# A table of decay powers made by four GpSimd copies across partitions instead of four on-chip transfers

## The chip, the cores and the metric

One NeuronCore of a Trainium2 chip runs the whole program in one launch. The metric is the device time in microseconds. The kernel before takes 454.82 us, the median of three runs (453.93, 455.42 and 454.82).

## What is computed

The reference is an RWKV-like attention with a decaying state, followed by an MLP with a GELU. For batch 4, 8 heads, 768 tokens and head size 48:

```python
for t in range(S):
    cur = einsum('bhd,bhe->bhde', u * k_t, v_t)
    y[:, :, t] = einsum('bhd,bhde->bhe', r_t, state + cur)
    state = w[None, :, :, None] * state + einsum('bhd,bhe->bhde', k_t, v_t)
x = y.transpose(0, 2, 1, 3).reshape(3072, 384)
h = x @ w_in                                  # 384 x 2048
out = (0.5 * h * (1 + erf(h / sqrt(2)))) @ w_out   # 2048 x 384
```

`w` is one decay per head and channel, so inside a chunk of tokens the decays are powers of `w`.

## The kernel before, in words

**Tiling.** The 768 tokens are six chunks of 128. The eight heads are four pairs, and a pair's two heads lie on partitions 0 to 47 and 64 to 111 of a tile with 112 partitions. A "group" is one chunk of one pair, over all four batches, so there are 24 groups. The four groups of the first chunk (`first_group`, `first_states`) have no state to read; the 20 later ones (`prepare`, `products`, `state`, `finish`) work on two half chunks of 64 tokens and with both orders of the two heads.

**The MLP.** For every chunk 16 blocks j of 128 hidden channels are worked through, 96 steps in all: nine matmuls of 128x512 into `Hp` or `O2` (`moe1`, L697), a gelu twice on ScalarE (L729 rounded, L730 full), their difference on VectorE (L731), and nine matmuls into `O0` to `O2` (`moe2`, L741). Nine, because every float32 factor is split into a high and a low part. The weights are split too, once, in the first steps: a load `raw` (L381), ScalarE's L396 and L399, VectorE's L401, ScalarE's cast `wh` (L405), VectorE's remainder `wl` (L408).

**The table of powers.** `W` (112 partitions, four pairs) holds for every channel w to the powers 0 to 64 (`powers`, L322 to L329), their inverses (`inverse`, L334, one reciprocal for each pair), and a second row of powers for the first chunk (`state_powers`). The later groups need the powers in another layout, and for both orders of the heads: `E[:, p, a, h, i]`. h = 0 has each head's own powers on its partitions. h = 1 has the other head's: those of partitions 64 to 111 go to 0 to 47, and back. `halves` (L365) fills it. E is read by L355 (TensorE transposes of it, from which ScalarE makes `WN2` at L358), by L559 (VectorE, the scaling of a later group's r and k) and by L664 (VectorE, the state).

**What sets the order.** The program gives each piece of work to a planner (`Plan.add`): an engine, an assumed duration, a due time, what it reads and writes. `Plan.run` carries due times back through the users, and `Plan.play` then simulates the engines and hands out, time after time, the ready piece that is due first. So an edit of one piece can move the instructions of every engine. Two of its rules matter here. First, GpSimd's work is kept apart from VectorE's work that is marked `port`: lines 169 to 174 add, to each GpSimd piece with a port, a wait for the last such VectorE piece that was handed out before it. Second, dummy matmuls (`heat`, L306) are put into TensorE's order where the planner foresees a gap before the first step of the MLP. SP's DMA queue is in the planner's order too; each transfer uses one of eight semaphores in turn and waits until the transfer that last used it has landed.

Of the kernel before, what the change touches and what calls it, by code (L numbers as in the profile page):

```python
# [21 lines left out]
B, H, S, D = 4, 8, 768, 48  # L22
# [8 lines left out]
HALF = 64  # L31
LP = 112
# [6 lines left out]
LATER = 10 ** 7  # L39
# [7 lines left out]
SWAP_DUE = 50000  # L47
ROUND = "a"
LOADS = (1, 2, 3, "w0", "w1", 4, "u", "w2", 5)
AT_LOADS, AT_E = 14000, 15000  # L50

SCALE = ("dd", "d", "d", "d")
PRODUCT = ("d", "d", "d", "d")
# [3 lines left out]
class Plan:  # L57
# [16 lines left out]
    def add(self, eng, ns, at, fn, r=(), w=(), port=False):  # L74
        n = len(self.ops)
        deps = set()
        for x in r:
            deps.add(self.writer.get(x))
            self.readers.setdefault(x, []).append(n)
        for x in w:  # L80
            deps.add(self.writer.get(x))
            deps.update(self.readers.pop(x, ()))
            self.writer[x] = n
        deps -= {None, n}
        self.ops.append((eng, ns, at, fn, deps, port or eng == "pool"))
        self.reads.append(set(r))
        self.writes.append(set(w))
        return n

    def dma(self, nbytes, at, fn, r=(), w=()):  # L90
        self.add("sp", nbytes, at, fn, r, w)
# [99 lines left out]
def rwkv_gelu_mlp(tc, rkT, rkv, wuT, uN, wmlp, r, k, vT, w, u, out):  # L191
    nc = tc.nc
    with ExitStack() as ctx:
# [7 lines left out]
        def sb(shape, dt, name, pool=None):  # L201
            return (pool or wk).tile(shape, dt, name=name)
# [19 lines left out]
        W = sb([LP, NP, KEYS + C], F32, "W", pro)  # L222
        WKs = W[:, :, KEYS:]
        E = sb([LP, NP, 2, 2, HALF], F32, "E")
# [27 lines left out]
        add, dma = plan.add, plan.dma  # L252
# [3 lines left out]
        pool = lambda n: 200 + n * 2.1  # L256
# [29 lines left out]
        for dst, src, x in ((diag2, diag, "diag"), (past2, past, "past")):  # L286
            for h in range(2):
                add("act", 245, LATER, lambda dst=dst, src=src, h=h: nc.scalar.copy(
                    out=dst[64 * h:64 * h + 64], in_=src[64 * h:64 * h + 64, 64 - 64 * h:128 - 64 * h]),
                    r=[x], w=[f"{x}2{h}"])  # L290
# [21 lines left out]
        for x in wa:  # L312
            add("act", act(2 * DM), LATER, lambda x=x: nc.scalar.copy(
                out=x.bitcast(F32).rearrange("p (a n) -> p a n", a=2),
                in_=zeros[:, 0:DM].bitcast(F32).unsqueeze(1).to_broadcast([128, 2, DM])), r=["zeros"], w=["wa"])
# [47 lines left out]


        def halves(src, dst, h):  # L365
            W2 = W[src].rearrange("l p (a i) -> l (p a) i", a=2)[:, :, 32:32 + HALF]
            nc.sync.dma_start(E[dst].rearrange("l p a h i -> l (p a) h i")[:, :, h], W2)

        every = [f"W{p}" for p in PAIRS] + ["P", "WKs"]
        for i, (src, dst, h) in enumerate(((slice(0, LP), slice(0, LP), 0), (slice(48, 64), slice(48, 64), 1),  # L370
                                           (slice(0, D), slice(64, LP), 1), (slice(64, LP), slice(0, D), 1))):
            dma(60000, AT_E, lambda src=src, dst=dst, h=h: halves(src, dst, h), r=every, w=[f"E{i}"])
        EVERY = [f"E{i}" for i in range(4)]
        add("pe", 560, LATER, lambda: flip(lambda p: E[:, p, 1].rearrange("l h i -> l (h i)")), r=EVERY + ["ident"], w=["O0"])
        add("act", 400, LATER, flipped(WN2), r=["O0"], w=["WN2"])
# [70 lines left out]
        def first_group(gi, at, XX, XB, y, YB):  # L446
# [8 lines left out]
            for i, e in enumerate(halves):  # L455
                nb = NB // len(halves)
                bs = slice(i * nb, i * nb + nb)
                mul = nc.vector.tensor_tensor if e == "d" else nc.gpsimd.tensor_tensor
                add("dve" if e == "d" else "pool", dve(256 * nb) if e == "d" else pool(256 * nb), LATER,
                    lambda mul=mul, bs=bs, nb=nb: mul(  # L460
                        out=t[:, :, bs], in0=T[gi][:LP, :, bs],
                        in1=W[:, p, 0:C].unsqueeze(1).unsqueeze(1).to_broadcast([LP, 2, nb, C]), op=ALU.mult),
                    r=["P", f"W{p}", f"T{gi}"], w=[f"{TR}{b}" for b in range(bs.start, bs.stop)], port=True)
# [545 lines left out]
```

## Time and profile before

| what | value |
| --- | --- |
| median of three runs | 454.82 us |
| the profiled execution | 453.82 us, its span 452.1 us |
| TensorE busy | 440.6 us, 97% of the span |
| VectorE busy | 229.4 us, 51% |
| ScalarE busy | 186.7 us, 41% |
| GpSimd busy | 68.5 us, 15% |

The span runs from the first to the last instruction; the rest of the execution's time lies around it. The shares are means over stages that differ: VectorE and ScalarE are nearly full in the first 80 us, while the weights are split, and have much room after that. In the slices of the page TensorE's row reads 7 9 8 8 and then 9 throughout.

### The profile page before, as it was taken

The page shows a single profiled execution, that of the slowest core. Times are in us where ns is not written, and L with a number is a line of the kernel's source. Part 1 is how long each engine was busy: PE and PEld are TensorE (multiplying, and loading weights), DVE is VectorE, ACT ScalarE, POOL GpSimd, SP SyncE. Part 2 cuts the span into 40 slices and gives each one's busy share as a digit, 9 for nine tenths or more (in the row PEclk, how much of TensorE's full clock was granted, in tenths as well). Part 3 has the DMA queues.
Part 4 walks back from the last instruction along what each step waited for, and adds up shares of the span by engine and source line. Part 5 has one row for each costly group of instructions (what it writes and reads, how often), then busy time and mean ns, then how long its engine had stood idle before and what let it go on. Part 6 is the DMA issues. An engine that isn't in the chain of part 4 may idle for free.

```text
span 452.1 us, 10289 instructions
## 1 busy us (share of the span) xinstructions
PE 440.6 (97%) x4525; PEld 379.4 (84%) x4525; DVE 229.4 (51%) x345; ACT 186.7 (41%) x333; POOL 68.5 (15%) x91
## 2 busy tenths in 40 slices
PE   7988999999999999999999999999999999999995
PEld 6767878888888888888888888888888888888885
DVE  7988979876353538253454545445425411211111
ACT  9998998533232223222233222323223222322221
POOL 1233011223101211102202202112022000000000
PEclk9999999999999999999999999999999999999999
DMA  8987864335031234030321411302503000100002
GB/s 300 362 336 226 292 222 174 112 113 171 1 113 45 68 113 146 26 106 5 113 80 73 131 54 59 112 25 87 171 1 112 15 0 13 70 1 1 1 0 75
DMA packets 15426, 46.60 MB, mean 103 GB/s; under 512 B 3664, under 2 KB 4048, under 8 KB 15376
## 3 DMA queue, kind: packets, MB, share of 16 engines
q1 hardware_dynamic: 15376, 45.88, 30.9%
q8 instruction: 37, 0.61, 0.6%
q14 instruction: 13, 0.11, 0.1%
HBM read 38.73 MB, written 4.72 MB: 96 GB/s over the span
## 4 chain that ended last, share of the span: by engine, by line
PE 78%; ACT 8%; DVE 6%; DMA 5%; issue 2%; POOL 1%; SPq 0%; ACTq 0%; POOLq 0%
PE Hp L697 36%; PE O L741 34%; DMA E<-W 2%; PE Y L607 2%; ACT wh L405 2%; ACT wa L396 2%; PE Y L635 2%; PE A L615 2%; ACT wb L399 1%; DVE wb L401 1%; DMA raw<-in_wmlp_dram 1%; PE Y L741 1%; PE A L624 1%; DMA T<-in_rkT_dram 1%; ACT gh L729 1%
## 5 line engine op out<-in xcount | busy, mean ns | idle before, releaser
L697 PE MATMUL Hp<-xx,wh 128*128 128x512 f32 x570 | 157.0, 383 | 0.4 <-ACT gf L730 0.4
L731 DVE TENSOR_TENSOR gl<-gf,gh 128x512 fp32r<-128x512 f32 x92 | 67.8, 737 | 139.5 <-ACT gf L730 138.8
L729 ACT ACTIVATE gh<-Hp 128x512 fp32r<-128x512 f32 x91 | 54.4, 598 | 190.2 <-PE Hp L697 190.1
L697 PEld LDWEIGHTS Hp<-xx,wh 128*128 128x128 f32 x570 | 105.4, 189 | 16.5 <-ACT gf L730 0.8
L741 PE MATMUL O<-gh,wh 128*128 128x512 f32 (+1 forms) x276 | 74.5, 377 | 3.3 <-ACT gh L729 2.5
L697 PE MATMUL Hp<-xx,wl 128*128 128x512 f32 x285 | 77.4, 379 | 0.0
L741 PE MATMUL O<-gl,wh 128*128 128x512 f32 (+1 forms) x276 | 74.1, 376 | 0.0
L741 PE MATMUL O<-gh,wl 128*128 128x512 f32 (+1 forms) x276 | 73.9, 375 | 0.0
L741 PEld LDWEIGHTS O<-gh,wh 128*128 128x128 f32 x276 | 51.6, 189 | 12.8 <-ACT gh L729 4.5
L697 PEld LDWEIGHTS Hp<-xx,wl 128*128 128x128 f32 x285 | 53.8, 189 | 7.6
L741 PEld LDWEIGHTS O<-gl,wh 128*128 128x128 f32 x276 | 51.2, 189 | 7.2 <-issue 0.3
L741 PEld LDWEIGHTS O<-gh,wl 128*128 128x128 f32 x276 | 51.3, 189 | 6.8
L730 ACT ACTIVATE gf<-Hp 128x512 f32<-128x512 f32 x95 | 56.4, 594 | 0.0
L562 POOL TENSOR_TENSOR Nb<-Nb 128x384 f32<-128x384 f32 x20 | 20.1, 1007 | 127.0 <-DMA Nb<-in_rkv_dram 81.3
L559 DVE TENSOR_TENSOR Tb<-Tb,E 112x1024 f32<-112x1024 f32 x20 | 25.0, 1252 | 3.0 <-DMA Tb<-in_rkT_dram 3.0
L565 POOL TENSOR_TENSOR Nb<-Nb,WN 128x384 f32<-128x384 f32 x20 | 20.8, 1038 | 28.1 <-DVE wl L408 17.3
L664 DVE SCALAR_TENSOR_TENSOR Sb<-Sa,E,A 48x192 f32<-48x192 f32 x40 | 16.5, 413 | 14.9 <-PE A L624 14.3
L434 ACT CAST xx<-Y 112x512 fp32r<-112x512 f32 x15 | 8.9, 592 | 36.3 <-PE Y L635 36.3
L568 POOL TENSOR_TENSOR Nb<-Nb,u_sb 128x384 f32<-128x384 f32 x20 | 21.3, 1064 | 6.7 <-DVE gl L731 6.7
L571 DVE TENSOR_REDUCE cs<-Nb 128x8 f32<-128x384 f32 x20 | 11.0, 552 | 21.4 <-POOL Nb L568 20.5
L396 ACT ACTIVATE wa<-raw 128x768 f16<-128x768 bf16 x16 | 18.9, 1182 | 0.2 <-DMA raw<-in_wmlp_dram 0.2
L399 ACT ACTIVATE wb<-raw 128x768 int32<-128x768 uint32 x16 | 18.6, 1187 | 0.2 <-DVE wl L408 0.2
(124 smaller groups left out, 371.1 us busy)
## 6 DMA issues: line engine op xcount, KB each, us to landing
raw<-in_wmlp_dram SPq DMA_DIRECT2D x16, 767.8 KB, 6.1
Nb<-in_rkv_dram SPq DMA_DIRECT2D x20, 576.0 KB, 5.5
Tb<-in_rkT_dram SPq DMA_DIRECT2D x20, 512.0 KB, 3.9
out_dram<-raw SPq DMA_DIRECT2D x5, 768.0 KB, 3.6
T<-in_rkT_dram SPq DMA_DIRECT2D x4, 512.0 KB, 5.2
xx<-x SPq DMA_DIRECT2D x30, 64.0 KB, 4.2
N<-in_rkv_dram SPq DMA_DIRECT2D x4, 384.0 KB, 7.0
out_dram<-raw SPq DMA_DIRECT2D x2, 256.0 KB, 3.9
```

The source lines that it names most:

```text
L396: add("act", 930, LATER, lambda: nc.scalar.activation(out=a.bitcast(F16).rearrange("p (n t) -> p n t", t=2)[:, :, 1], in_=top.bitcast(BF16 ...
L399: add("act", 815, LATER, lambda: nc.scalar.activation(out=b, in_=rest.bitcast(U32), func=AF.Copy, scale=2.0 ** -13), r=[R_], w=[B_])
L559: add("dve", 1140, LATER, lambda: nc.vector.tensor_tensor(out=flat, in0=flat, in1=E[:, p, 0].rearrange("l h i -> l (h i)").unsqueeze(1).to ...
L562: add("pool", pool(DM), LATER, lambda: nc.gpsimd.tensor_tensor(out=n[:, 0], in0=n[:, 0], in1=n[:, 1], op=ALU.mult), r=[NK], w=[NR])
L565: add("pool", pool(DM), LATER, lambda: nc.gpsimd.tensor_tensor(out=kn, in0=kn, in1=WN2[:, p].rearrange("s j d -> s (j d)").unsqueeze(1).to ...
L568: add("pool", pool(DM), LATER, lambda: nc.gpsimd.tensor_tensor(out=n[:, 0], in0=n[:, 0], in1=u_sb[:, p, :].unsqueeze(1).to_broadcast([C, N ...
L664: add("dve", 430, at, lambda l=l, x=x: nc.vector.scalar_tensor_tensor(out=out[quarter(1 - x)], in0=src[l], scalar=E[l, p, 1, h, 32:33], in ...
L697: nc.tensor.matmul(dst, lhsT=wt[j][:, 0, k_ * 128:(k_ + 1) * 128], rhs=pairs(x[:, a, k_, :]), start=start and k_ == ks[0], stop=stop and k ...
L729: add("act", 480, LATER, lambda: nc.scalar.activation(out=high, in_=dst, func=AF.Gelu, scale=256.0), r=[H_], w=[GH])
L730: add("act", 480, LATER, lambda: nc.scalar.activation(out=gf, in_=dst, func=AF.Gelu, scale=256.0), r=[H_], w=["gf"])
L731: add("dve", dve(512), LATER, lambda: nc.vector.tensor_tensor(out=low, in0=gf, in1=high.bitcast(F32), op=ALU.subtract), r=["gf", GH], w=[G ...
L741: nc.tensor.matmul(dst[:, a:b], lhsT=wt[j][:, 1, d * 128:(d + 1) * 128], rhs=pairs(gt)[:, a // 2:b // 2], start=(j == 0 and n == 0), stop= ...
```

## The change

The four transfers of L367, given to SP's queue with a fixed due time, become four GpSimd copies. Each reads `W` and writes one part of E, across partitions where h = 1. The second part is copied from a wider block, partitions 32 to 63 in place of 48 to 63, so that it overlaps the third on 32 to 47; the third therefore waits for the second. The last two change places. The pieces have no due time of their own but get it from their users, and an assumed duration of 700 ns.

```diff
-AT_LOADS, AT_E = 14000, 15000
+AT_LOADS = 14000
...
         def halves(src, dst, h):
-            W2 = W[src].rearrange("l p (a i) -> l (p a) i", a=2)[:, :, 32:32 + HALF]
-            nc.sync.dma_start(E[dst].rearrange("l p a h i -> l (p a) h i")[:, :, h], W2)
+            W2 = W[src].rearrange("l p (a i) -> l p a i", a=2)[:, :, :, 32:32 + HALF]
+            return nc.gpsimd.tensor_copy(out=E[dst, :, :, h], in_=W2)
 
         every = [f"W{p}" for p in PAIRS] + ["P", "WKs"]
-        for i, (src, dst, h) in enumerate(((slice(0, LP), slice(0, LP), 0), (slice(48, 64), slice(48, 64), 1),
-                                           (slice(0, D), slice(64, LP), 1), (slice(64, LP), slice(0, D), 1))):
-            dma(60000, AT_E, lambda src=src, dst=dst, h=h: halves(src, dst, h), r=every, w=[f"E{i}"])
+        for i, (src, dst, h) in enumerate(((slice(0, LP), slice(0, LP), 0), (slice(32, 64), slice(32, 64), 1),
+                                           (slice(64, LP), slice(0, D), 1), (slice(0, D), slice(64, LP), 1))):
+            add("pool", 700, LATER, lambda src=src, dst=dst, h=h: halves(src, dst, h), r=every,
+                w=[f"E{i}"] + ["E1"] * (i == 2))
```

The planner then hands out a different order on every engine. Lines behind the edit are one higher in the new file (L471 is L472, L697 is L698); the text keeps the old numbers.

GpSimd, at the start of the program, before. `ident` is the identity for transposes, `N` the first chunk's k and v, `Nb` a later group's.

```order
L279 AFFINE_SELECT ident<-ones 128x128
L517 TENSOR_TENSOR N_107<-N_107,WN 128x384
L517 TENSOR_TENSOR N_108<-N_108,WN 128x384
L517 TENSOR_TENSOR N_109<-N_109,WN 128x384
L517 TENSOR_TENSOR N_110<-N_110,WN 128x384
L562 TENSOR_TENSOR Nb_111<-Nb_111 128x384
L565 TENSOR_TENSOR Nb_111<-Nb_111,WN_92 128x384
```

The same place of GpSimd now:

```order
L279 AFFINE_SELECT ident<-ones 128x128
L367 COPY E<-W 32x8x64
L367 COPY E<-W 112x8x64
L367 COPY E<-W 48x8x64 x2
L518 TENSOR_TENSOR N_107<-N_107,WN 128x384
L518 TENSOR_TENSOR N_108<-N_108,WN 128x384
L518 TENSOR_TENSOR N_109<-N_109,WN 128x384
L518 TENSOR_TENSOR N_110<-N_110,WN 128x384
L563 TENSOR_TENSOR Nb_111<-Nb_111 128x384
L563 TENSOR_TENSOR Nb_112<-Nb_112 128x384
```

The four copies stand ahead of the four decay products of the first chunk. In the new program's list of waits the first copy waits for VectorE's L421 and the second for VectorE's L401; the four products wait in turn for the copies, L408 of the first weight block, and the first and the second L559.

VectorE, from the scaling of the second group to the first weight block, before:

```order
L334 RECIPROCAL W<-W 112x64 x3
L460 TENSOR_TENSOR Ts_99<-T_93,W 112x2x256 x2
L466 TENSOR_TENSOR RK_104<-T_94 112x512
L460 TENSOR_TENSOR Ts_100<-T_94,W 112x1024
L490 COPY_PREDICATED Am_113<-past,A 128x1024
L466 TENSOR_TENSOR RK_105<-T_95 112x512
L466 TENSOR_TENSOR RK_106<-T_96 112x512
L460 TENSOR_TENSOR Ts_101<-T_95,W 112x1024
L435 TENSOR_TENSOR x_123<-O_72,x_123 112x512
L490 COPY_PREDICATED Am_114<-past,Y 128x1024
L460 TENSOR_TENSOR Ts_102<-T_96,W 112x1024
L421 TENSOR_TENSOR Am_116<-diag,cs_120 128x512
```

The same place of VectorE now:

```order
L334 RECIPROCAL W<-W 112x64 x2
L461 TENSOR_TENSOR Ts_100<-T_94,W 112x1024
L467 TENSOR_TENSOR RK_105<-T_95 112x512
L491 COPY_PREDICATED Am_113<-past,A 128x1024
L461 TENSOR_TENSOR Ts_101<-T_95,W 112x1024
L467 TENSOR_TENSOR RK_106<-T_96 112x512
L491 COPY_PREDICATED Am_114<-past,Y 128x1024
L436 TENSOR_TENSOR x_123<-O_72,x_123 112x512
L334 RECIPROCAL W<-W 112x64
L461 TENSOR_TENSOR Ts_102<-T_96,W 112x1024
L422 TENSOR_TENSOR Am_116<-diag,cs_120 128x512
L402 ISA wb_134<-wb_134,wa_132 128x1536
```

Three reciprocals that ran in one go are now a pair and a single one, and the last stands behind the second L490.

TensorE, from the last scores of the first chunk to the first steps of the MLP, before. `O_70` takes the transposes of E, `A` the states' gains, `Hp` and `O_72` the first two steps.

```order
L498 MATMUL O_72<-x_123,spread 128x512 x2
L355 MATMUL O_70<-ident,E 128x112 x4
L306 MATMUL Hp<-zeros 128x512
L504 MATMUL O_72<-Am_115,N_109 48x128 x8
L498 MATMUL O_71<-x_123,spread 128x512 x2
L526 MATMUL A<-N_107 48x48 x8
L526 MATMUL A<-N_108 48x48 x8
L504 MATMUL O_71<-Am_116,N_110 48x128 x8
L697 MATMUL Hp<-xx_121,wh_74 128x512
```

The same place of TensorE now:

```order
L306 MATMUL Hp<-zeros 128x512 x5
L505 MATMUL O_72<-Am_115,N_109 48x128 x8
L499 MATMUL O_71<-x_123,spread 128x512 x2
L355 MATMUL O_70<-ident,E 128x112 x4
L505 MATMUL O_71<-Am_116,N_110 48x128 x8
L698 MATMUL Hp<-xx_121,wh_74 128x512
L698 MATMUL Hp<-xx_121,wl_78 128x512
L698 MATMUL Hp<-xx_121,wh_74 128x512 x2
L698 MATMUL Hp<-xx_121,wl_78 128x512
L698 MATMUL Hp<-xx_121,wh_74 128x512
L527 MATMUL A<-N_107 48x48 x8
L527 MATMUL A<-N_108 48x48 x8
```

The transposes of E have moved behind one L504 and stand directly ahead of the last one, and the first 16 gain products have moved behind the first six L697.

## Rows read from the trace of the kernel before

**Rows 1.** Busy time by stretch: stretch, length, PE, PEld, DVE, ACT, POOL, clock, DMA share, GB/s
```profile
8.00:16.00 8.00, 7.87 (x91) 6.75 (x90) 7.86 (x10) 7.69 (x27) 0.00 (x0) 1.00 1.03 408
23.60:78.00 54.40, 50.72 (x553) 41.69 (x550) 48.39 (x65) 50.82 (x67) 11.29 (x13) 1.00 0.72 252
78.00:96.00 18.00, 17.89 (x320) 15.37 (x319) 13.22 (x20) 10.00 (x16) 5.53 (x7) 1.00 0.29 83
96.00:440.00 344.00, 343.89 (x3395) 299.35 (x3394) 145.50 (x226) 101.90 (x187) 46.93 (x60) 1.00 0.21 66
```

**Rows 2.** TensorE's waits, 23.6 to 96 us (us in total, times, longest)
```profile
PE O L741 <- ACT gh L729: 2.5, 4, 1.0
PE O L741 <- ACT gf L730: 0.8, 1, 0.8
PE Hp L697 <- ACT gf L730: 0.4, 1, 0.4
```

**Rows 3.** Timeline of TensorE, 18 to 31 us (start, length, instruction)
```profile
19.27 0.55 PE L355 MATMUL O<-ident,E 112*128 112x112 f32 x4
19.59 0.48 PE L306 MATMUL Hp<-zeros 128*128 128x512 f32 x1
...
21.95 0.92 PE L526 MATMUL A<-N 128*48 128x48 f32 x32
22.71 1.04 PE L504 MATMUL O<-Am,N 128*48 128x128 f32 x16
23.68 0.48 PE L697 MATMUL Hp<-xx,wh 128*128 128x512 f32 x1
...
25.18 0.93 PE L526 MATMUL A<-N 128*48 128x48 f32 x32
26.03 0.48 PE L697 MATMUL Hp<-xx,wh 128*128 128x512 f32 x1
...
28.49 0.81 PE L697 MATMUL O<-xx,wl 128*128 128x512 f32 x3
29.14 0.81 PE L697 MATMUL O<-xx,wh 128*128 128x512 f32 x3
```

**Rows 4.** Two pieces of the chain of waits, and the transfers of E
```profile
7.88 10.55 DMA E<-W
18.45 6.13 DMA raw<-in_wmlp_dram
...
E<-W SPq DMA_DIRECT2D x1, 224.0 KB, 10.6
E<-W SPq DMA_DIRECT2D x2, 96.0 KB, 6.7
...
E<-W SPq DMA_DIRECT2D x1, 32.0 KB, 9.9
```

**Rows 5.** Timeline of GpSimd
```profile
0.81 0.20 POOL L276 MEMSET ones<- 128x128 f32 x1 [0.29 <-POOLq L996]
1.09 0.29 POOL L279 TENSOR_SCALAR_AFFINE_SELECT diag<-ones 128x128 f32<-128x128 f32 x1
...
18.73 2.95 POOL L517 TENSOR_TENSOR N<-N,WN 128x384 f32<-128x384 f32 x3 [16.86 <-DMA E<-W]
23.00 1.00 POOL L517 TENSOR_TENSOR N<-N,WN 128x384 f32<-128x384 f32 x1 [1.31 <-DVE wl L408]
...
40.52 0.09 POOL L645 MEMSET done<- 1x1 f32 x1 [1.53 <-PE Y L607]
```

**Rows 6.** Timeline of VectorE
```profile
16.87 0.69 DVE L421 TENSOR_TENSOR Am<-diag,cs 128x512 f32<-128x512 f32 x1
17.69 0.96 DVE L401 CUSTOM_DVE_ANT_0 wb<-wb,wa 128x1536 uint16<-128x1536 uint16 x1
...
20.71 1.37 DVE L490 COPY_PREDICATED Am<-past,Y 128x1024 f32<-128x1024 uint32 x1
...
23.45 1.37 DVE L401 CUSTOM_DVE_ANT_0 wb<-wb,wa 128x1536 uint16<-128x1536 uint16 x1
```

**Rows 7.** Timeline of ScalarE
```profile
24.60 1.16 ACT L396 ACTIVATE wa<-raw 128x768 f16<-128x768 bf16 x1 [0.21 <-DMA raw<-in_wmlp_dram]
25.60 0.82 ACT L405 CAST wh<-wb 128x768 fp32r<-128x768 f32 x1
```

## The prediction

> **What bounds the kernel now.** I read the busy shares by stretch first, to see where TensorE is the bound, then who makes TensorE wait, then the start of the program instruction by instruction, because the change touches only that. By stretch [rows 1], TensorE is busy 343.89 of 344.00 us from 96 to 440, and 17.89 of 18.00 from 78 to 96. From 23.6 to 78 it is busy 50.72 of 54.40, so 3.7 us idle; ScalarE is busy 50.82 there and VectorE 48.39, since the weights are split then. Three rows name what TensorE waits for [rows 2]: 2.5 + 0.8 + 0.4 = 3.7 us, all for ScalarE's gelu (L729, L730). So the end is set by three things: when the first product of the MLP (L697) starts, which is 23.68 us [rows 3]; how much TensorE work stands behind that point; and the idle time behind it. From 78 us on every microsecond that TensorE is behind shows up whole at the end. The granted clock is 1.00 in all these stretches [rows 1], the upper of its two levels, so it plays no part.
>
> The transfers that the change takes away look worse than they are. The chain of waits holds 10.55 us of E<-W from 7.88 on [rows 4], but that is a transfer standing in a full queue: the 16 DMA engines are busy 1.03 of the time from 8 to 16 us and move 408 GB/s [rows 1]. And nobody stood waiting for the landed E: the transposes of it run at 19.27, right behind the row before them [rows 3]. The row of GpSimd's first long wait, 16.86 us, puts it down to E [rows 5]; but that product neither reads nor writes E, it starts 0.08 us after VectorE's L401 (17.69 + 0.96 = 18.65, [rows 6]), which it is made to wait for on account of the shared port.
>
> **The change part by part.** *Removed: four transfers.* They are 224 + 32 + 2 x 96 = 448 KB [rows 4]; at 408 GB/s that is 1.1 us of a full DMA system. So everything queued behind lands about 1.1 us sooner, the third weight load at 23.5 in place of 18.45 + 6.13 = 24.58 [rows 4]. What it buys is small: ScalarE waited 0.21 us for that load [rows 7]. I take 0.2 us, and it is inside the next steps. SP's queue is no longer held at 7.88 to wait for W; the loads behind could be issued earlier, but into the same full queue.
>
> *Added: four copies on GpSimd, 512 columns each.* The trace has no copy on GpSimd. From below: a write of one column takes 0.09 and of 128 columns 0.20 [rows 5], so 0.11 / 127 = 0.9 ns a column, 0.09 + 512 x 0.0009 = 0.55 us. From above: the two-input product, 128x384 in about 1.0 us [rows 5], 2.6 ns a column, 1.34 us. The select at L279 reads one input as a copy does, 0.29 for 128 columns [rows 5]: (0.29 - 0.09) / 127 = 1.6 ns, so 0.9 us. I take 0.9, and 0.55 to 1.34 for the range. GPSIMD Engine Reference, Performance versus the Vector engine, in the Trainium skill, gives 769 ns for 512 elements at its best loop; by that E would be complete 0.5 us sooner and the sum below 0.3 us smaller.
>
> *When they run.* They need all four reciprocals, and the last of these is moved behind the second L490 (the order of VectorE). More than that, a GpSimd instruction with the port waits for the last VectorE port instruction handed out before it: the first copy waits for L421, the second for L401. VectorE has the same instructions ahead of L421 as before and was busy 7.86 of 8.00 us there [rows 1], so L421 ends about where it did, 16.87 + 0.69 = 17.56 [rows 6]. Copy 1 runs 17.6 to 18.5. L401 would start at 17.69, and is held off by it: in the trace L401 takes 1.37 in place of 0.96 while a GpSimd product is on from 23.00 to 24.00 [rows 5, 6], and ends 0.82 after it. So L401 ends at 18.5 + 0.85 = 19.4, and copies 2 to 4 end at 19.4 + 3 x 0.9 = 22.1. E is complete at 22.1, where before it was there at 19.2.
>
> SBUF — State Buffer, Who interferes with whom, in the Trainium skill, says that an instruction of VectorE with two SBUF inputs contends with any GpSimd instruction that reads SBUF. The trace shows it only for products with two inputs. If copies with one input are free of it, E is complete 0.5 us sooner and the sum is 0.3 us smaller; by the rule it stays.
>
> *Who waits for them.* On TensorE the transposes of E now stand directly ahead of the last L504 and the first L697. L504 needs L490, which ends at 20.71 + 1.37 = 22.08 [rows 6], so even with instant copies the first L697 isn't before 22.1 + 0.97 = 23.1 (22.71 to 23.68 is the L504, [rows 3]). With E at 22.1, 0.35 for the transposes (19.27 to 19.59 and a little) and 0.97: 23.4, which is 0.3 sooner than 23.68. But the 16 gain products (L526) that ran ahead of it at 21.95 [rows 3] now run behind it. On GpSimd the four decay products (L517), which began at 18.73 [rows 5], begin at about 22.1, in the middle of VectorE's L408 and L401 for the first two weight blocks. Two of them lie across these, each costing VectorE about the 0.41 us of [rows 6]. So wh of the second block, cast at 25.60 + 0.82 = 26.42 [rows 7] before, is there at about 26.5; TensorE, which is through its six L697 and 16 gains at 23.4 + 6 x 0.216 + 0.76 = 25.5, waits 1.0 us for it. (0.216 is a third of 28.49 to 29.14; 0.76 is 21.95 to 22.71, [rows 3].) It then has six more L697, 1.3 us, to 27.8; the second block's wl comes out of the next L408, behind L559 and a third decay product, at 28.5 (27.4 if the product stays clear of it). TensorE waits 0.7 us more and reaches the product with wl of the second block at 28.5.
>
> That is the point to compare: in the trace it is at 28.49 [rows 3]. Same time, but before TensorE had by then also done 16 more gain products (25.18 to 26.03, 0.85) and two L741 (2 x 0.216 = 0.43): 1.3 us of work that now lies behind. **First term: +1.3 us.**
>
> *Behind 28.5.* Here VectorE's and ScalarE's instructions are the same in kind and number, in another order. The new order of ScalarE has several places where weight casts and splits stand ahead of a gelu (two casts and a split between one gelu pair and the next), and a gelu is what TensorE waits for. I went through both orders with the row durations, each instruction starting when its engine and its inputs are free; the old order comes out within 0.5 us of the trace up to 70 us, and the new one has 0.9 us more idle on TensorE. That is an estimate. Its bounds: if TensorE's lateness is all taken out of the idle time (there are about 3 us left of the 3.7), the term is -1.3; if the waits grow by half, +1.8. **Second term: +0.9 us.**
>
> Sum: +2.2 us. The profiled execution would go from 453.82 (span 452.1 and 1.7 around it) to 456.0; it lay 1.0 below the median of 454.82, so the forecast for the median is 457.0.
>
> **The rivals.** *Slower still, by dear copies.* If a copy takes 1.34 us, E is complete 4 x 0.44 = 1.8 us later, and since the transposes stand in TensorE's row ahead of the first L697, all of it counts: 458.8. It decides from about 0.8 us a copy on (17.6 + 4 x 0.8 + 0.85 + 0.35 = 22.0); below that L490 hides them. For it speaks that the product next in line takes 2.6 ns a column; against, that a copy has one input. GPSIMD Engine Reference, Instruction dispatch, in the Trainium skill, adds some 6 us to the first call of freshly loaded code, which would make it about 463; the first L517 started with no such delay [rows 5].
>
> *No change: ScalarE sets the pace.* It is busy 50.82 of 54.40 us from 23.6 to 78. If the splits there follow each other as before, TensorE's 1.3 us come out of its idle time: 454.8. Against it: two of its waits are made by the new order itself, and behind 78 us nothing is left to give back.
>
> *Faster: the early loads win.* If E is complete by 20.7 (copies of 0.55 us) and the weight loads, 1.1 us sooner, move the splits of the third block on as much, then the first L697 is at 23.1 (-0.6), and 1.1 of the 3.7 us idle goes while the gains cost 0.85: -0.9 us, 453.9. For it speaks the full DMA system; against, that ScalarE waited for a load only 0.21 us.
>
> **How the numbers follow.** A measurement of this kernel can tell about 0.3%, 1.4 us. Forecast (+1.4 to +3.5 us): 0.53. Dear copies: 0.13. No change: 0.22. Faster: 0.12. So slower 0.66, same 0.22, faster 0.12. The forecast's own range is 456.2 to 458.3; the range for 8 in 10 takes in part of no change and most of the dear copies: 454.5 to 459.2.
>
> **What would show it.** Four GpSimd copies of about 0.9 us from 17.6 on, with L401 stretched beside the first; E complete near 22; the first L697 at 23.1 to 23.6; the gain products right behind its first six; TensorE's idle time from 23.6 to 78 up from 3.7 to 5 us or more, with new waits for the casts of the second block (L405, L408). It is wrong if the copies run before 17 us, if that idle time falls, or if the first L697 slips past 24.5.

## The result, and the profile after

The changed kernel takes 458.03 us (median of 4, 457.36 to 458.37) against 454.39 (453.93 to 455.42): ratio 1.0074, 95% interval 1.0062 to 1.0086. It is slower by 0.7%, clear of noise, inside the range, 1.0 us above the forecast of 457.0; the forecast change was 2.2 us, the measured one is 3.6. The profiled execution is 457.36, its span 455.4, 3.3 us longer than before's 452.1. In what follows every line of the changed program is one higher than in the text so far (L697 is L698).

Busy time by stretch, the columns of [rows 1]:

```profile
23.60:78.00 54.40, 49.48 (x570) 39.98 (x570) 47.06 (x62) 50.02 (x66) 12.80 (x15) 1.00 0.68 238
78.00:96.00 18.00, 17.67 (x200) 14.98 (x200) 14.89 (x21) 10.41 (x16) 3.17 (x5) 1.00 0.23 71
96.00:440.00 344.00, 343.89 (x3513) 299.49 (x3512) 146.51 (x227) 101.54 (x186) 49.43 (x63) 1.00 0.21 66
```

From 23.6 to 78 TensorE is now idle for 54.40 - 49.48 = 4.9 us in place of 3.7, and 0.3 from 78 to 96 in place of 0.1. Behind 96 TensorE's busy time is the same to the hundredth. Whom TensorE waits for, 22 to 96 us (total, times, longest):

```profile
PE O L742 <- ACT gh L730: 1.7, 3, 1.2
PE O L742 <- DVE gl L732: 1.5, 2, 1.2
PE Hp L698 <- ACT gf L731: 1.2, 2, 0.9
PE O L698 <- DVE wl L409: 0.5, 1, 0.5
PE O L742 <- ACT gf L731: 0.2, 1, 0.2
```

Against [rows 2] two names are new: VectorE's `gl`, and `wl` of the second weight block. GpSimd's start:

```profile
17.60 0.60 POOL L367 COPY E<-W 32x512 f32<-32x512 f32 x1 [15.72 <-DVE Am L422]
19.15 1.94 POOL L367 COPY E<-W 112x512 f32<-112x512 f32 x3 [0.95 <-DVE wb L402]
21.18 1.02 POOL L518 TENSOR_TENSOR N<-N,WN 128x384 f32<-128x384 f32 x1
23.09 1.00 POOL L518 TENSOR_TENSOR N<-N,WN 128x384 f32<-128x384 f32 x1 [0.89 <-DMA raw<-in_wmlp_dram]
26.12 1.02 POOL L518 TENSOR_TENSOR N<-N,WN 128x384 f32<-128x384 f32 x1 [2.03 <-DVE Tb L560]
```

The copies take 0.60 to 0.61 us each, some 0.05 apart, and E is complete at 21.1. The decay products, three of them back to back from 18.73 before [rows 5], now start 2 to 5 us apart (the fourth at 30.81, not shown). VectorE there:

```profile
17.85 1.17 DVE L402 CUSTOM_DVE_ANT_0 wb<-wb,wa 128x1536 uint16<-128x1536 uint16 x1 [0.40 <-ACT wb L400]
...
20.78 1.37 DVE L491 COPY_PREDICATED Am<-past,Y 128x1024 f32<-128x1024 uint32 x1
...
26.56 1.38 DVE L409 TENSOR_TENSOR wl<-wb,wh 128x768 fp32r<-128x768 f32 x1
```

TensorE, to set beside [rows 3]:

```profile
21.93 0.54 PE L355 MATMUL O<-ident,E 112*128 112x112 f32 x4
22.41 1.08 PE L505 MATMUL O<-Am,N 128*48 128x128 f32 x16
23.42 0.48 PE L698 MATMUL Hp<-xx,wh 128*128 128x512 f32 x1
...
24.91 0.93 PE L527 MATMUL A<-N 128*48 128x48 f32 x32
25.97 0.92 PE L698 MATMUL O<-xx,wh 128*128 128x512 f32 x3
...
28.00 0.92 PE L698 MATMUL O<-xx,wl 128*128 128x512 f32 x3 [0.47 <-DVE wl L409]
```

TensorE's last product, before and after:

```profile
446.81 0.28 PE L741 MATMUL Y<-xx,wh 128*128 128x256 f32 x1
...
449.44 0.28 PE L742 MATMUL Y<-xx,wh 128*128 128x256 f32 x1
```

It ends at 446.81 + 0.28 = 447.09 before and at 449.44 + 0.28 = 449.72 now. That is 2.6 of the 3.3 us. The other 0.7 lie behind the last product, in SP's issues of the output transfers. Before:

```profile
445.87 1.78 SPq L783 DMA_DIRECT2D out_dram<-raw  x1
447.76 0.37 SPq L783 DMA_DIRECT2D out_dram<-Nb  x1
```

After:

```profile
448.51 2.47 SPq L784 DMA_DIRECT2D out_dram<-raw  x1
451.09 0.56 SPq L784 DMA_DIRECT2D out_dram<-Nb  x1
```

The same third issue starts 2.64 us later and takes 0.69 longer; the last issue waits behind it on SP.

### The profile page after: what moved, and what is told of

Same layout as the page of the kernel before. It is cut to its first block, busy times and chain, and to the rows that moved or that the text cites. A ratio compares the mean times of both kernels' runs of the same rounds, so it can differ in the third digit from the quotient of the medians.

```text
span 455.4 us, 10292 instructions
## 1 busy us (share of the span) xinstructions
PE 442.3 (97%) x4527; PEld 380.7 (84%) x4527; DVE 231.4 (51%) x345; ACT 187.0 (41%) x333; POOL 70.6 (15%) x95
## 4 chain that ended last, share of the span: by engine, by line
PE 83%; ACT 7%; DMA 5%; DVE 2%; issue 1%; SPq 1%; DVEq 0%
PE Hp L698 38%; PE O L742 37%; DMA raw<-in_wmlp_dram 3%; PE Y L608 2%; ACT wa L397 2%; PE Y L636 2%; PE A L616 2%; DMA N<-in_rkv_dram 2%; ACT wb L400 1%; PE A L625 1%; DMA Tb<-in_rkT_dram 1%; ACT wh L406 1%; PE Y L742 1%; ACT gf L731 1%; ACT gh L730 1%
## 5 line engine op out<-in xcount | busy, mean ns | idle before, releaser
L698 PE MATMUL Hp<-xx,wh 128*128 128x512 f32 x570 | 156.9, 383 | 1.2 <-ACT gf L731 1.2
L732 DVE TENSOR_TENSOR gl<-gf,gh 128x512 fp32r<-128x512 f32 x92 | 69.8, 759 | 139.2 <-ACT gf L731 138.6
L698 PEld LDWEIGHTS Hp<-xx,wh 128*128 128x128 f32 x570 | 105.2, 189 | 17.2 <-ACT gf L731 2.1
L698 PE MATMUL Hp<-xx,wl 128*128 128x512 f32 x285 | 77.5, 380 | 0.0
L742 PE MATMUL O<-gh,wh 128*128 128x512 f32 (+1 forms) x276 | 74.3, 376 | 1.9 <-ACT gh L730 1.7
L742 PE MATMUL O<-gl,wh 128*128 128x512 f32 (+1 forms) x276 | 74.1, 376 | 1.5 <-DVE gl L732 1.5
L742 PE MATMUL O<-gh,wl 128*128 128x512 f32 (+1 forms) x276 | 73.9, 375 | 0.0
L742 PEld LDWEIGHTS O<-gh,wh 128*128 128x128 f32 x276 | 51.8, 189 | 10.9 <-ACT gh L730 3.2
L698 PEld LDWEIGHTS Hp<-xx,wl 128*128 128x128 f32 x285 | 53.6, 189 | 7.7
L742 PEld LDWEIGHTS O<-gl,wh 128*128 128x128 f32 x276 | 51.2, 189 | 9.3 <-DVE gl L732 2.3
L742 PEld LDWEIGHTS O<-gh,wl 128*128 128x128 f32 x276 | 51.3, 189 | 6.8
L560 DVE TENSOR_TENSOR Tb<-Tb,E 112x1024 f32<-112x1024 f32 x20 | 24.6, 1231 | 3.3 <-DMA Tb<-in_rkT_dram 3.3
L569 POOL TENSOR_TENSOR Nb<-Nb,u_sb 128x384 f32<-128x384 f32 x20 | 20.1, 1004 | 9.5 <-DVE gl L732 5.0
L400 ACT ACTIVATE wb<-raw 128x768 int32<-128x768 uint32 x16 | 18.6, 1161 | 1.5 <-DVE wl L409 1.3
```

The source lines that it names most:

```text
L400: add("act", 815, LATER, lambda: nc.scalar.activation(out=b, in_=rest.bitcast(U32), func=AF.Copy, scale=2.0 ** -13), r=[R_], w=[B_])
L560: add("dve", 1140, LATER, lambda: nc.vector.tensor_tensor(out=flat, in0=flat, in1=E[:, p, 0].rearrange("l h i -> l (h i)").unsqueeze(1).to ...
L569: add("pool", pool(DM), LATER, lambda: nc.gpsimd.tensor_tensor(out=n[:, 0], in0=n[:, 0], in1=u_sb[:, p, :].unsqueeze(1).to_broadcast([C, N ...
L698: nc.tensor.matmul(dst, lhsT=wt[j][:, 0, k_ * 128:(k_ + 1) * 128], rhs=pairs(x[:, a, k_, :]), start=start and k_ == ks[0], stop=stop and k ...
L732: add("dve", dve(512), LATER, lambda: nc.vector.tensor_tensor(out=low, in0=gf, in1=high.bitcast(F32), op=ALU.subtract), r=["gf", GH], w=[G ...
L742: nc.tensor.matmul(dst[:, a:b], lhsT=wt[j][:, 1, d * 128:(d + 1) * 128], rhs=pairs(gt)[:, a // 2:b // 2], start=(j == 0 and n == 0), stop= ...
```

## The experiments

The theory ("order theory" in the expectations) is the prediction's, sharpened: the loss is in the order that the planner hands out, and the copies' own time is nearly hidden. The rival ("copy theory" or "duration theory"): the copies' time on GpSimd, and the port that it shares with VectorE, delay everything behind them. "Idle" is TensorE's from 23.6 to 440 us, the three stretches above added (a wait before 23.6 is not in it); "end" is the end of its last product. The expectations count idle time in another way, by the distances between TensorE's starts from the first product on, and put before at 4.9 to 5.0 and after at 6.7 to 6.8: compare their differences with those of the table. "End" and "idle" come from one profiled execution of each kernel, the medians from 4 to 23 runs. Each ratio is to runs of before made beside that kernel, whose medians are 454.31 to 454.40.

| kernel | median us | ratio to before, 95% | copies | first L697 | idle | end |
| --- | --- | --- | --- | --- | --- | --- |
| before | 454.39 | | none | 23.68 | 3.9 | 447.09 |
| after | 458.03 | 1.0074 (1.0062 to 1.0086) | 17.6 to 21.1 | 23.42 | 5.4 | 449.72 |
| copies_old_order | 454.84 | 1.0005 (0.9994 to 1.0016) | 7.6 to 12.0 | 24.87 | 3.8 | 447.90 |
| told_900 | 463.76 | 1.0221 (1.0194 to 1.0248) | 17.7 to 21.2 | 23.52 | 9.5 | 455.29 |
| due_12000 | 452.42 | 0.9957 (0.994 to 0.9973) | 11.3 to 15.7 | 24.27 | 2.4 | 445.34 |
| due_15000 | 454.24 | 0.9997 (0.9988 to 1.0006) | 10.1 to 15.3 | 23.68 | 3.2 | 446.89 |
| transfers_due_12000 | 453.51 | 0.9981 (0.9968 to 0.9993) | none | 24.54 | 3.1 | 446.84 |
| copies_tiny | 457.50 | 1.0070 (1.0051 to 1.0089) | 17.5 to 19.5 | 23.07 | 5.6 | 449.69 |
| copies_twice | 462.87 | 1.0183 (1.0149 to 1.0217) | 17.5 to 24.8 | 27.70 | 6.5 | 455.18 |
| copies_twice_warm | 459.41 | 1.0108 (1.0091 to 1.0125) | 17.5 to 24.8 | 26.44 | 5.2 | 452.28 |

Only after and copies_tiny number their lines one higher.

**The copies in the old order.** Against before; the planner still reckons with transfers, so TensorE, VectorE and ScalarE have before's order. The copies carry no wait for VectorE's `port` pieces here, since the planner takes them for transfers.

```diff
-            nc.sync.dma_start(E[dst].rearrange("l p a h i -> l (p a) h i")[:, :, h], W2)
+            nc.gpsimd.tensor_copy(out=E[dst, :, :, h], in_=W2)
...
             dma(60000, AT_E, lambda src=src, dst=dst, h=h: halves(src, dst, h), r=every, w=[f"E{i}"])
```

> The four GpSimd copies, but every engine's instructions in the order of the kernel before (the planner still reckons with transfers; only what is issued is a copy). The order theory (the loss comes from the new order of VectorE, ScalarE and TensorE behind 24 us): the idle time of TensorE behind the first L697 stays as before, 4.9 us by its starts or less, and what remains is what the copies themselves cost in the place where they now run, 7 to 12 us, the fullest stretch of VectorE: up to 4 x 0.6 = 2.4 us there, first L697 at about 25.4 in place of 23.7, the end +1.3 us. The copy theory (GpSimd's copies and the port are the loss wherever the rest stands): idle time as in the changed kernel, 6.7 us, and the end at least +2.6.

```profile
7.57 4.44 POOL L367 COPY E<-W 112x512 f32<-112x512 f32 x4 [5.69 <-ACT past L288]
```

The copies run 10 us earlier, beside a full VectorE, and stretch to 1.1 us each on average. The first L697 comes 1.2 us later and TensorE's end 0.8; I had put them at 1.7 and 1.3. TensorE's idle time is 3.8, before's 3.9, and not after's 5.4. The median is 0.4 above before's; by the interval the replacement itself, without another order, is worth between -0.3 and +0.7 us, which can't be told from nothing.

**Another reckoned duration.** Against after, one number that only the planner reads:

```diff
-            add("pool", 700, LATER, lambda src=src, dst=dst, h=h: halves(src, dst, h), r=every,
+            add("pool", 900, LATER, lambda src=src, dst=dst, h=h: halves(src, dst, h), r=every,
...
```

> The changed kernel, with one number of the planner changed: a copy is reckoned at 900 ns in place of 700. The same instructions, the same copies at the same place. Order theory: the copies run at 17.6 to 21.1 as in the changed kernel and the first L697 is where it was, yet the time moves by several us, because the later order differs: about +3.5 against the changed kernel (+6 against before). Copy theory: within 0.5 us of the changed kernel.

Copies and first product stand where they stand in after, to 0.1 us, but the time is 5.7 us longer, where I had expected 3.5. Two of TensorE's waits there, one from the list of 22 to 110 us and one from its timeline:

```profile
PE A L624 <- POOL Nb L565: 1.6, 1, 1.6
...
110.92 0.45 PE L697 MATMUL Hp<-xx,wh 128*128 128x512 f32 x1 [2.72 <-DMA xx<-x]
```

And the stretches around the first of them:

```profile
42.00:44.00 2.00, 0.44 (x37) 0.37 (x32) 1.27 (x2) 1.98 (x4) 0.99 (x1) 1.00 0.67 178
44.00:46.00 2.00, 1.91 (x25) 1.48 (x14) 1.94 (x5) 2.00 (x4) 0.93 (x1) 0.67 0.87 269
46.00:48.00 2.00, 2.00 (x7) 1.53 (x6) 1.91 (x5) 1.45 (x2) 1.05 (x2) 0.50 0.79 292
```

Behind a stretch in which TensorE was busy 0.44 of 2.00 us the granted clock (third column from the right) is 0.67 and then 0.50, the lower of its two levels, 1.2 GHz. Nine L697 take 3.7 us there, from 44.30 to 47.99, and not 9 x 0.216 = 1.9. So of the 5.7 us some 4 are waits (idle 9.5 against 5.4) and 1.8 the clock that fell behind one of them. The largest wait, 2.72, is for a transfer of a later chunk's `xx` that this order issues at 107.04, just ahead of its use; after has no such wait. All this comes with the order: apart from it the two programs differ by one dummy matmul (six L306 in place of five at 18.6).

**Earlier due times.** Against after:

```diff
-            add("pool", 700, LATER, lambda src=src, dst=dst, h=h: halves(src, dst, h), r=every,
+            add("pool", 700, 12000, lambda src=src, dst=dst, h=h: halves(src, dst, h), r=every,
...
```

> The changed kernel, with a due time of 12000 ns for the copies in place of none, so the reciprocals and the copies are handed out early (the transfers had 15000). Order theory: the four reciprocals run in one go again, the copies end near 15 us, E waits for nobody, the first L697 at about 23.8 and TensorE's idle time behind it about 3 us in place of 6.7: about -2 us against before, -4 to -5 against the changed kernel. Copy theory: the copies cost the same GpSimd time and stand beside more of VectorE's work, so no better than the changed kernel.

```profile
23.60:78.00 54.40, 52.14 (x688) 43.38 (x685) 51.41 (x70) 51.89 (x69) 12.31 (x15) 1.00 0.76 262
78.00:96.00 18.00, 18.00 (x203) 15.54 (x202) 15.40 (x23) 9.35 (x15) 3.07 (x4) 1.00 0.24 72
```

This is the fastest of all, 0.43% under before, with its first product 0.6 us *later* than before's: what counts is the 2.3 us of idle from 23.6 to 78, and none from 78 to 96. With 15000, the due time that the transfers had:

> The copies of after with the due time that the transfers had (15000), in place of the one that follows from their users. Order theory: going through this order with the durations of the traces gives -0.9 against before, between before and due_12000: 453.6 (452.9 to 454.3), idle behind the first product 4 to 4.5 us. If due_12000 was a lucky single case and copies cost by themselves, it is 456 or more.

454.24: at the upper end of the interval that I gave, and the same as before. So due_12000 is not explained by copies that run early: here they end 0.5 us sooner still.

**The transfers with another due time.** Against before:

```diff
-AT_LOADS, AT_E = 14000, 15000
+AT_LOADS, AT_E = 14000, 12000
```

> The kernel before, with the due time of its four transfers at 12000 instead of 15000, nothing else: no copy at all, only another order handed out. Order theory: any number that the planner reads moves the time by a microsecond or so in either direction; going through this order with the durations of before gives -0.6: 453.8 (453.2 to 454.4). If the order matters only where the copies are, it is 454.4 with the idle time of before, 5.0. The stretch from TensorE's last product to the end should be 5.0, as in before, if the four transfers have a part in it, and 5.4 to 5.7 if not.

0.8 us faster by the medians, without any copy (in the profiled execution the last product ends only 0.25 sooner). A number that changes only the order, and with it one dummy matmul, moves the old kernel, too, by about what the theory gave. The guess on the end of the program falls: due_15000 has no such transfers, its last product ends at 446.89 in a span of 451.9, and its third output issue took 0.40 us:

```profile
445.68 0.40 SPq L783 DMA_DIRECT2D out_dram<-raw  x1
```

From last product to the end of the span it was 4.9 to 5.7 us in all ten. Why that issue takes 0.4 to 2.5 us stays open, and so does whether one kernel has the same issue time in every execution.

**Copies of one column.** Against after; this leaves out nearly all of the table, and sets E to zero once at the start:

```diff
-        add("pool", 290, 4, lambda: select(ident, 0, -1, ALU.is_equal), r=["ones"], w=["ident"])
+        add("pool", 290, 4, lambda: [select(ident, 0, -1, ALU.is_equal), nc.gpsimd.memset(E, 0.0)][0], r=["ones"], w=["ident"])
...
-            return nc.gpsimd.tensor_copy(out=E[dst, :, :, h], in_=W2)
+            return nc.gpsimd.tensor_copy(out=E[dst, 0:1, 0:1, h, 0:1], in_=W2[:, 0:1, 0:1, 0:1])
```

> Same order as after, but each of the four copies writes one column only, and E is zeroed once by GpSimd at about 2 us, where it idles; this leaves out nearly all of the table. It takes 4 x 0.5 = 2.0 us of GpSimd's work from the place where it stood, and the product beside which the first copy runs is no longer stretched. Order theory: the first L697 is held by L490 on VectorE and not by the copies, TensorE's waits stay where they are: 458.0, from 457.3 to 458.5, idle behind the first product 6.8 us. Duration theory (the copies' 2.4 us are what GpSimd's later products and the casts behind them are late by): at least half of the 3.3 us comes back, 456.3 or less.

457.50. This is the sharpest of the tests: GpSimd's first decay product starts 1.6 us sooner, VectorE's L402 is back at 0.96, and of the 3.6 us 0.5 come back by the medians (0.2 by the ratios), less than the two intervals can tell. TensorE's waits show why:

```profile
PE O L742 <- ACT gh L730: 1.7, 3, 1.1
PE Hp L698 <- ACT gf L731: 1.7, 3, 1.0
PE O L742 <- DVE gl L732: 1.0, 1, 1.0
PE O L742 <- ACT gf L731: 0.5, 1, 0.5
PE O L698 <- ACT wh L406: 0.5, 1, 0.5
```

Four of the five are after's waits, to within half a microsecond in each; the fifth is at the same block, for `wh` in place of `wl`. The first L698 comes 0.35 us sooner than in after, and that is lost again where TensorE next waits for a gelu. This product, in after and here:

```profile
31.05 0.48 PE L742 MATMUL O<-gh,wh 128*128 128x512 f32 x1 [0.19 <-ACT gf L731]
...
31.04 0.48 PE L742 MATMUL O<-gh,wh 128*128 128x512 f32 x1 [0.55 <-ACT gf L731]
```

TensorE's end is the same, 449.69 against 449.72. The duration theory, 456.3 or less, falls.

**Copies issued twice, and with TensorE kept at work.** Against after, and the second against the first:

```diff
-            return nc.gpsimd.tensor_copy(out=E[dst, :, :, h], in_=W2)
+            return [nc.gpsimd.tensor_copy(out=E[dst, :, :, h], in_=W2) for _ in range(2)][0]
...
-        add("pe", 560, LATER, lambda: flip(lambda p: E[:, p, 1].rearrange("l h i -> l (h i)")), r=EVERY + ["ident"], w=["O0"])
+        add("pe", 560, LATER, lambda: ([heat(O[0]) for _ in range(12)], flip(lambda p: E[:, p, 1].rearrange("l h i -> l (h i)"))), r=EVERY + ["ident"], w=["O0"])
```

> The changed kernel in its own order, each copy issued twice (the second repeats the first), so eight copies. It prices a dear copy: by the prediction's rival, all that is beyond 0.8 us a copy goes to the end. With 2 x 0.61 + 0.05 = 1.27 us for each pair: E complete about 3 us later, the first L697 at about 26.3 in place of 23.4 and the end +2.8 against the changed kernel, of which the idle time behind gives a little back. If the copies were hidden instead: within 0.5 us of the changed kernel.

> copies_twice with 12 products of zeros on TensorE ahead of the transposes of E, into the bank that these write: 2.6 us of work in the 2.9 us in which TensorE stood waiting for E. Clock theory: the copies alone cost +2.8 over after, and the other 2.0 us of copies_twice came from the 6.8 us at the lower clock: with TensorE kept at work the granted clock stays 1.00, the first L697 is at 26.3 instead of 27.70, and the time 460.9 (460.2 to 461.5). If the 2.0 us are later casts and not the clock, it stays at 462.9.

copies_twice came out 2.0 us dearer than expected, its first L697 at 27.70 and not 26.3:

```profile
22.00:24.00 2.00, 0.00 (x0) 0.00 (x0) 2.00 (x4) 0.30 (x1) 1.90 (x3) 0.93 1.04 427
24.00:28.00 4.00, 3.12 (x21) 2.47 (x22) 1.58 (x2) 1.65 (x3) 3.91 (x4) 0.50 0.99 413
28.00:31.00 3.00, 3.00 (x25) 1.99 (x26) 2.52 (x3) 1.93 (x3) 0.86 (x1) 0.57 0.07 20
```

With twelve products of zeros in that hole:

```profile
22.00:24.00 2.00, 2.00 (x10) 1.65 (x10) 2.00 (x4) 0.30 (x1) 1.90 (x3) 1.00 1.02 421
24.00:28.00 4.00, 3.82 (x32) 2.59 (x32) 2.13 (x3) 2.47 (x4) 3.91 (x4) 1.00 0.95 394
```

The clock stays at 1.00, the first L697 is at 26.44, and 3.5 us are gone (459.41), more than the 2.0 that I put down to the clock and below the interval that I gave; where the other 1.5 come from is not shown. So the four extra copies by themselves cost 1.4 us by the medians and not 2.8. By the profiled ends of TensorE it is 452.28 - 449.72 = 2.6; how much is left open by that, but both say that copies on TensorE's path cost, while taking nearly all of after's copying away (copies_tiny) brings back no more than can be told.

## Why the prediction was right, step by step

**The start: right in place, wrong in size.** The copies began at 17.60 as forecast and the first L698 came at 23.42 against 23.4, because L491 sets it (20.78 + 1.37 = 22.15, then the L505 at 22.41). In copies_tiny L491 ends at 21.80 and the L505 starts at 22.06, the same 0.26 us behind. But a copy took 0.61 us, near the lower bound of 0.55, and not 0.9: the write of 1 and of 128 columns in [rows 5] was the better guide than the select. GPSIMD Engine Reference, Performance versus the Vector engine, in the Trainium skill, gives 769 ns for 512 elements at its best loop; this trace is below it. The stretched L402 was there, 1.17 against 0.96 [rows 6], with a one-input copy on GpSimd from 17.60 to 18.20; in copies_tiny, where that copy is over before the L402 starts, it takes 0.96. SBUF — State Buffer, Who interferes with whom, in the Trainium skill, has a VectorE instruction with two SBUF inputs contend with a GpSimd instruction that reads SBUF; the trace agrees with it here, where before it showed it for two-input products only.

**First term, +1.3: measured +0.8.** The product with `wl` of the second block is reached at 28.00 and not 28.49, with the same 1.28 us of gains and L742 still to do: 1.28 - 0.49 = 0.8. The new waits ahead of it are those that I named, but 0.47 us for L409 in place of 0.7, and 0.3 for the cast in place of 1.0, since E was complete 1.0 us sooner. copies_tiny gets there at 27.63, so at this point 0.4 of the 0.8 was the copies' time, and the other 0.4 the order. The copies' 0.4 is gone again at 31.05.

**Second term, +0.9: measured +1.8.** This is the mis-sized one. TensorE's end moved by 2.6, of which 0.8 were there at 28. It lies at my upper bound of 1.8. Two waits near 60 us are 2.4 us together, where the longest of before was 1.0 [rows 2]. What ScalarE does ahead of the second of them:

```profile
58.53 0.84 ACT L406 CAST wh<-wb 128x768 fp32r<-128x768 f32 x1 [0.27 <-DVE wb L402]
59.27 1.28 ACT L397 ACTIVATE wa<-raw 128x768 f16<-128x768 bf16 x1
60.39 0.87 ACT L406 CAST wh<-wb 128x768 fp32r<-128x768 f32 x1
61.11 1.26 ACT L397 ACTIVATE wa<-raw 128x768 f16<-128x768 bf16 x1
62.23 0.87 ACT L406 CAST wh<-wb 128x768 fp32r<-128x768 f32 x1
62.95 0.64 ACT L730 ACTIVATE gh<-Hp 128x512 fp32r<-128x512 f32 x1
```

Three casts and two splits stand ahead of a gelu that TensorE waits for. The two waits in TensorE's row, the first of them for VectorE, and what VectorE and GpSimd do ahead of that:

```profile
57.68 0.92 PE L742 MATMUL O<-gl,wh 128*128 128x512 f32 x3 [1.19 <-DVE gl L732]
...
63.65 0.70 PE L742 MATMUL O<-gh,wh 128*128 128x512 f32 x2 [1.17 <-ACT gh L730]
...
56.31 1.31 DVE L732 TENSOR_TENSOR gl<-gf,gh 128x512 fp32r<-128x512 f32 x1
...
56.08 0.99 POOL L563 TENSOR_TENSOR Nb<-Nb 128x384 f32<-128x384 f32 x1 [7.25 <-DMA Nb<-in_rkv_dram]
```

For the second wait I had named the cause (casts and splits between one gelu pair and the next). The first I had not: VectorE does the work of a later group (L560 and L672, from 54.55 to 56.42) ahead of the gelu's remainder L732, which then takes 1.31 us beside a GpSimd product where it takes 0.68 at 58.41. The term was priced by a walk through the order that was itself up to 0.5 us off the trace of before. The forecasts for the other orders missed by 0.0 (due_12000), 0.3 (transfers_due_12000), 0.6 (due_15000) and 2.2 us (told_900), so that this one came within 1.0 us of the median is in part luck. That these rows make the waits is read from the trace; no run moved these instructions alone.

**The end: not in the sum.** +0.7 in the profiled execution, the third output issue. I took the 5.0 us behind the last product as fixed. Whether the runs without a profile have it too is not shown.

So 0.8 + 1.8 + 0.7 = 3.3 where I had 2.2; the medians moved by 3.6.

**The rivals.** Dear copies fell by the first row, at 0.61 us. No change needed TensorE's deficit to come out of its idle time; the idle time grew. Faster, by early loads: the third load did land 1.1 us sooner, but ScalarE had come to it sooner too and waited 0.48 us in place of 0.21 [rows 7]:

```profile
23.47 1.25 ACT L397 ACTIVATE wa<-raw 128x768 f16<-128x768 bf16 x1 [0.48 <-DMA raw<-in_wmlp_dram]
```

What the forecast did not have is what copies_old_order, told_900 and due_12000 show together: with the same four copies the time goes from 2.0 us under before to 9.4 over it, by the order and what follows from it (1.8 us of the 9.4 is the lower clock). The sign came out right because the prediction went through the very order that was handed out, not because copies on GpSimd would be slower than transfers: no run shows that they are.

## What to carry to other kernels

Where a planner sets the order, price an edit twice: once in the order of before (here +0.4 us, nothing that can be told), and once as another order, which is worth several times as much and has no sign until it is walked through row by row. A number that only the planner reads (a reckoned duration, a due time) is a knob of its own: trying two values of it took this change from 0.74% slower to 0.43% faster, and it moved the kernel without the change, too. A first product that comes earlier buys nothing while a later wait takes it back: compare idle time up to the last stretch that is not full, not the start.

## What was not expected of the hardware

- A GpSimd copy of 512 columns takes 0.60 to 0.61 us on 32, 48 or 112 partitions and across partitions alike, but 0.86 to 1.23 us beside a full VectorE with no wait between the two (4.44 us for four in copies_old_order).
- A wait can cost twice: after 2.9 us without a product in copies_twice, the granted clock read 0.50 and later 0.57 over the seven microseconds behind it. In told_900 it fell behind a wait of 1.56 us. Twelve products of zeros that nobody reads made copies_twice 3.5 us faster.
- The same transfer issue on SP at the end of the program took 0.40 us in one kernel's profile and 2.47 in another's, with the same output to write.
